# Linear attention and a two-layer network in one kernel: where block 0's first part ends

## The chip, the cores and the metric

One core of a Trainium2 chip runs the kernel. The metric is the device time of one execution in microseconds (us), median of the runs; lower is better. Engines are named as the profile names them: PE is TensorE (its matmuls; PEld its weight loads), DVE is VectorE, ACT is ScalarE, POOL is GpSimd, SP issues the DMAs.

## The reference

The kernel computes attention with exponential feature maps and feeds its output to a two-layer network. For 8 batches of 8 heads, 576 tokens and a head width of 64:

```python
def phi(x):
    proj = np.einsum('bhsd,df->bhsf', x, w_phi)
    proj = proj - np.max(np.abs(proj), axis=-1, keepdims=True)
    return np.concatenate([np.exp(proj), np.exp(-proj)], axis=-1)
q_p, k_p = (phi(q), phi(k))
kv = np.einsum('bhsf,bhsd->bhfd', k_p, v)
z = np.sum(k_p, axis=2)
num = np.einsum('bhsf,bhfd->bhsd', q_p, kv)
den = np.einsum('bhsf,bhf->bhs', q_p, z)[..., None] + 1e-06
x = (num / den).transpose(0, 2, 1, 3).reshape(B * S, H * D)
h = x @ w_in
g = np.maximum(0.01 * h, h)
return g @ w_out
```

The network has 4608 tokens, a width of 512 and 2048 hidden features. w_in and w_out arrive as 64-bit floats.

## The kernel before, in words

**Attention** goes by head pairs, i = 4 x batch + pair, 32 in all. A pair has a k phase (k_phase: projections, exponentials, the matrix kv) and a q phase (token_q_phase for pairs 4 to 7, q_phase from 8 on: projections, exponentials, numerator and denominator, division). The result is written to `ring`, which holds two batches. The last step of a pair's q phase is POOL's multiplication `ring<-ring,mb`. Pairs 0 to 3 (batch 0) have functions of their own that run first. From pair 4 on the generator `attention()` gives the k phase of pair i and the q phase of pair i - 1 in turns, and `advance(goal)` draws from it.

**The network** works on 18 blocks of 256 tokens. `split(i)` copies a block out of `ring` in two parts, xh on ACT and the rest xl on POOL; both tiles exist once, so a block's split waits until layer 1 of the block before it has been read. A step (i, ft) is block i with one of 16 weight groups of 128 hidden features: `layer1` has 12 matmuls of 256 columns (L601, L602, L604; w0h and w0l are the two parts of w_in), then ACT and DVE make gh and gl (L607, L69, L609), and `layer2` has 6 matmuls of 512 columns into two accumulators (L623 to L625, w1h and w1l for w_out). Layer 2 is written three steps behind layer 1 (LAG). Tokens 0 to 575 are batch 0, so blocks 0 and 1 need batch 0 alone, block 2 needs pairs 4 to 7 and block 4 (tokens 1024 to 1279) pairs 8 to 11.

**The weights** are prepared on the chip by `load_weights`: 32 pieces of 512 KB, w_in and w_out in turns by group, are loaded, turned from 64-bit to 32-bit numbers and split in two parts by DVE, ACT and copies (L160 to L169). The last step of a piece is `w0l<-ql,w0h` or `w1l<-ql,w1h` on DVE (L74).

**Order.** Block 0 is cut in two. Its first CUT steps come first, then the 16 steps of block 1, then the rest of block 0, then blocks 2 to 17. After the first part `layer2` copies the two half sums from the accumulators to a tile (held, tag ks, L629 to L633), and after the last part they are added (L636). The lines that set this:

```python
steps = [(i, ft) for i in range(2, NBLK) for ft in range(NFT)]
steps = [(0, ft) for ft in range(CUT)] + [(1, ft) for ft in range(NFT)] + [(0, ft) for ft in range(CUT, NFT)] + steps
split(0)
for n, (i, ft) in enumerate(steps):
    layer1(i, ft)
    advance(min(room(n // NFT + 1), NP * (1 + (n + 1) / NFT * T / S) + 2))
    if n + 1 < len(steps) and steps[n + 1][0] != i:
        advance(math.ceil((steps[n + 1][0] + 1) * T / S) * NP)
        split(steps[n + 1][0])
    if n >= LAG:
        layer2(*steps[n - LAG])
```

The order on each engine is not that of the code. A scheduler orders the instructions when the program is built, by priorities: batch 0 first (PF, PU), then the rest of attention (PA), then the weights (PW), then the network (0). Each engine then runs its list strictly in that order, so an instruction that waits holds up all behind it.

Of the kernel before, what the change touches and what calls it, by code (L numbers as in the profile page):

```python
# [27 lines left out]
NTOK = B * S  # L28
NBLK = NTOK // T
LAG = 3  # L30
CUT = 8
NN = 8
NK = 8
NF = 12
# [12 lines left out]
def attention_moe_kernel(ctx: ExitStack, tc: tile.TileContext, q, k, v, vt, w_phi, w_in, w_out, out):  # L47
# [538 lines left out]
    def split(i):  # L586
        for d in range(NP):
            t0 = 0
            while t0 < T:
                c = (i * T + t0) % (2 * S)  # L590
                n = min(T - t0, S - c % S)
                x = ring[:, c // S, d, c % S : c % S + n]
                t1 = t0 + n
                copy_("xh", xh[:, d, t0:t1], x)
                tt_("xl", xl[:, d, t0:t1], x, xh[:, d, t0:t1].bitcast(F32), ALU.subtract)
                t0 = t1
# [17 lines left out]
    def layer2(i, ft, half=range(TT)):  # L614
        first, last = (ft in (0, CUT), ft in (CUT - 1, NFT - 1)) if i == 0 else (ft == 0, ft == NFT - 1)
        if first and half[0] == 0:
            for t in range(TT):
                accs[i, t] = pt("acc")
        gh, gl = gs[i, ft]
        for t in half:  # L620
            ts = slice(t * P, t * P + P)
            a = accs[i, t]
            nc.tensor.matmul(a, lhsT=gh[:, ts], rhs=weight(1, "h", ft), start=first, stop=False)  # L623
            nc.tensor.matmul(a, lhsT=gh[:, ts], rhs=weight(1, "l", ft), start=False, stop=False)  # L624
            nc.tensor.matmul(a, lhsT=gl[:, ts], rhs=weight(1, "h", ft), start=False, stop=last)  # L625
        if not last:
            return
        for t in half:
            if ft == CUT - 1:  # L629
                if t == 0:  # L630
                    held[0] = st([P, TT, DM], F32, "ks")
                copy_("o", held[0][:, t], accs[i, t])
                continue  # L633
            o = st([P, DM], F32, "ek" if i == NBLK - 1 and t else "o")
            if i == 0:
                nc.vector.tensor_tensor(o, accs[i, t], held[0][:, t], op=ALU.add)  # L636
            else:
                copy_("o", o, accs[i, t])
            r = i * T + t * P
            nc.sync.dma_start(out[r : r + P, :], o)  # L640
# [29 lines left out]
# [3 lines that stand above are left out]
# [47 lines left out]
```

## Time and profile before

| | before |
|---|---|
| median of 3 runs | 1194.11 us (1193.7 to 1196.47) |
| profiled execution | 1196.45 us, its span 1194.7 us |
| PE busy | 1164.5 us, 97% |
| DVE busy | 755.9 us, 63% |
| ACT busy | 833.5 us, 70% |
| POOL busy | 417.5 us, 35% |
| mean granted PE clock | 0.994 |

The times are those of one profiled execution unless said otherwise. A row of a timeline gives start, length, engine, line, operation and tiles (output<-inputs), and in brackets how long the engine had been idle and what ended that. A row of the stage windows gives the busy time of each engine in a stretch, with the number of instructions, the granted clock of PE (1.00 is full), the share of the DMA engines and GB/s. Line 69, 71 or 74 is that of a helper that records copies and two-input operations, so there the tile says what is meant.

### The profile page before, as it was taken

The page shows a single profiled execution, that of the slowest core. Times are in us where ns is not written, and L with a number is a line of the kernel's source. Part 1 is how long each engine was busy: PE and PEld are TensorE (multiplying, and loading weights), DVE is VectorE, ACT ScalarE, POOL GpSimd, SP SyncE. Part 2 cuts the span into 40 slices and gives each one's busy share as a digit, 9 for nine tenths or more (in the row PEclk, how much of TensorE's full clock was granted, in tenths as well). Part 3 has the DMA queues.
Part 4 walks back from the last instruction along what each step waited for, and adds up shares of the span by engine and source line. Part 5 has one row for each costly group of instructions (what it writes and reads, how often), then busy time and mean ns, then how long its engine had stood idle before and what let it go on. Part 6 is the DMA issues. An engine that isn't in the chain of part 4 may idle for free.

```text
span 1194.7 us, 21190 instructions
## 1 busy us (share of the span) xinstructions
PE 1164.5 (97%) x7576; PEld 1045.5 (88%) x7576; DVE 755.9 (63%) x1510; ACT 833.5 (70%) x2108; POOL 417.5 (35%) x422
## 2 busy tenths in 40 slices
PE   8899999999998999999999999999999999999998
PEld 5687888899897989889899999998999999988987
DVE  4899883566767777677787777726777776111111
ACT  4898884667777787878788888837787877432232
POOL 0111011345454444545455454604454544110000
PEclk9899999999998999999999999999999999999999
DMA  7334532111201111110111111101011100000000
GB/s 208 90 101 142 152 114 59 40 42 31 60 22 50 32 50 31 41 30 22 50 31 50 32 49 32 49 12 37 23 50 32 49 1 19 1 18 19 1 19 18
DMA packets 62778, 57.01 MB, mean 48 GB/s; under 512 B 45136, under 2 KB 46288, under 8 KB 62672
## 3 DMA queue, kind: packets, MB, share of 16 engines
q1 hardware_dynamic: 62672, 55.65, 16.4%
q8 instruction: 60, 0.98, 0.4%
q14 instruction: 46, 0.38, 0.1%
HBM read 46.20 MB, written 9.44 MB: 47 GB/s over the span
## 4 chain that ended last, share of the span: by engine, by line
PE 82%; DVE 8%; ACT 5%; issue 2%; DMA 1%; POOL 1%; SPq 0%; DVEq 0%; ACTq 0%; POOLq 0%
PE h L601 10%; PE h L604 10%; PE h L602 10%; PE acc L623 10%; PE acc L625 10%; PE acc L624 10%; PE c L211 7%; PE a L302 2%; PE a L420 2%; PE a L418 2%; PE a L417 2%; PE a L231 2%; PE a L333 1%; PE a L377 1%; PE a L378 1%
## 5 line engine op out<-in xcount | busy, mean ns | idle before, releaser
L601 PE MATMUL h<-xh,w0h 128*128 128x256 f32 x1152 | 296.3, 287 | 5.9 <-DVE gl L609 4.9
L602 PE MATMUL h<-xh,w0l 128*128 128x256 f32 x1152 | 290.9, 282 | 0.0
L609 DVE TENSOR_TENSOR gl<-h,gh 128x256 fp32r<-128x256 f32 x288 | 118.7, 416 | 245.9 <-ACT gh L69 220.6
L623 PE MATMUL acc<-w1h,gh 128*128 128x512 f32 x576 | 229.6, 399 | 6.4 <-ACT gh L69 6.3
L601 PEld LDWEIGHTS h<-xh,w0h 128*128 128x128 f32 x1152 | 218.0, 189 | 17.0 <-DVE gl L609 8.0
L624 PE MATMUL acc<-w1l,gh 128*128 128x512 f32 x576 | 227.7, 395 | 0.0
L602 PEld LDWEIGHTS h<-xh,w0l 128*128 128x128 f32 x1152 | 217.9, 189 | 7.0 <-issue 0.4
L607 ACT ACTIVATE h<-h 128x256 f32<-128x256 f32 x288 | 105.3, 368 | 155.0 <-PE h L604 152.0
L625 PE MATMUL acc<-w1h,gl 128*128 128x512 f32 x576 | 204.4, 396 | 0.0
L604 PE MATMUL h<-xl,w0h 128*128 128x256 f32 x1152 | 200.3, 283 | 0.0
L74 POOL TENSOR_TENSOR ql<-eq,qh 128x576 fp32r<-128x576 f32 x96 | 146.5, 1539 | 73.6 <-ACT qh L69 51.0
L604 PEld LDWEIGHTS h<-xl,w0h 128*128 128x128 f32 x1152 | 164.5, 189 | 1.1 <-issue 0.4
L74 POOL TENSOR_TENSOR kpl<-ek,kph 128x512 fp32r<-128x512 f32 x72 | 96.6, 1342 | 146.9 <-PE c L211 67.2
L623 PEld LDWEIGHTS acc<-w1h,gh 128*128 128x128 f32 x576 | 108.4, 188 | 27.7 <-ACT gh L69 8.9
L624 PEld LDWEIGHTS acc<-w1l,gh 128*128 128x128 f32 x576 | 108.4, 188 | 18.0
L69 ACT CAST gh<-h 128x256 fp32r<-128x256 f32 x288 | 105.1, 371 | 25.6 <-PE acc L624 20.0
L74 POOL TENSOR_TENSOR xl<-ring,xh 128x256 fp32r<-128x256 f32 (+3 forms) x100 | 62.6, 655 | 162.1 <-PE h L604 131.6
L74 POOL TENSOR_TENSOR ring<-ring,mb 128x576 f32<-128x576 f32 (+2 forms) x45 | 49.8, 1108 | 192.9 <-DVE mb L559 39.2
L625 PEld LDWEIGHTS acc<-w1h,gl 128*128 128x128 f32 x576 | 99.3, 189 | 8.1
L249 ACT ACTIVATE ek<-pmk 128x256 f32<-128x256 f32 (+1 forms) x128 | 53.3, 417 | 33.5 <-POOL kpl L74 17.3
L199 DVE TENSOR_TENSOR ks<-rk,ks 64x576 fp32r<-64x576 f32 x40 | 44.5, 1112 | 30.5 <-ACT ks L69 29.9
L211 PE MATMUL c<-kph,vh 128*66 128x256 f32 x240 | 62.1, 281 | 0.7 <-ACT kph L69 0.7
(214 smaller groups left out, 2257.8 us busy)
## 6 DMA issues: line engine op xcount, KB each, us to landing
out_dram<-o SPq DMA_DIRECT2D x35, 256.0 KB, 2.1
rk<-in_k_dram SPq DMA_DIRECT2D x29, 288.0 KB, 2.8
ring<-in_w_in_dram SPq DMA_DIRECT2D x16, 512.0 KB, 3.6
qh<-in_w_out_dram SPq DMA_DIRECT2D x16, 512.0 KB, 3.7
rq<-in_q_dram SPq DMA_DIRECT2D x28, 288.0 KB, 3.0
rv<-in_v_dram SPq DMA_DIRECT2D x29, 256.0 KB, 3.5
rv<-in_vt_dram SPq DMA_DIRECT2D x58, 32.0 KB, 3.0
fr<-in_k_dram SPq DMA_DIRECT2D x2, 288.0 KB, 3.4
```

Source lines behind the costliest of these rows:

```text
L69: nc.scalar.copy(o, i)
L74: (nc.vector if pick(key) == "v" else nc.gpsimd).tensor_tensor(o, a, b, op=op)
L211: nc.tensor.matmul(kvp[0 : lt.shape[1], 256 * j : 256 * j + 256], lhsT=lt, rhs=rt, start=first and j == 0, stop=last, skip_group_check=True)
L249: nc.scalar.activation(ek[r, :, 0:F], pmk[r, 2 * s : 2 * s + 2], AF.Exp)
L601: nc.tensor.matmul(ph, lhsT=weight(0, "h", ft)[:, d * P : d * P + P], rhs=xh[:, d], start=d == 0, stop=False)
L602: nc.tensor.matmul(ph, lhsT=weight(0, "l", ft)[:, d * P : d * P + P], rhs=xh[:, d], start=False, stop=False)
L604: nc.tensor.matmul(ph, lhsT=weight(0, "h", ft)[:, d * P : d * P + P], rhs=xl[:, d], start=False, stop=d == NP - 1)
L607: nc.scalar.activation(ph, ph, AF.Prelu, alpha=0.01)
L609: nc.vector.tensor_tensor(gl, ph, gh.bitcast(F32), op=ALU.subtract)
L623: nc.tensor.matmul(a, lhsT=gh[:, ts], rhs=weight(1, "h", ft), start=first, stop=False)
L624: nc.tensor.matmul(a, lhsT=gh[:, ts], rhs=weight(1, "l", ft), start=False, stop=False)
L625: nc.tensor.matmul(a, lhsT=gl[:, ts], rhs=weight(1, "h", ft), start=False, stop=last)
```

## The change

Block 0's first part has twelve weight groups instead of eight:

```diff
-CUT = 8
+CUT = 12
```

The steps are the same 288. Before they went (0,0) to (0,7), (1,0) to (1,15), (0,8) to (0,15), (2,0) and on. Now they go (0,0) to (0,11), (1,0) to (1,15), (0,12) to (0,15), (2,0) and on. The half sums are put aside after group 11 instead of 7. The scheduler makes a new order of it on every engine; PE's is the same up to the end of (0,7) and again from head pair 25 on.

On PE, behind (0,7), stood the first step of block 1 (w0h_616 is the tile of w_in's groups 0 to 3, w1h_721 that of w_out's groups 4 to 7), layer 2 of an earlier step, and soon the next step:

```order
L604 MATMUL h<-xl,w0h_616 128x256 x4
L623 MATMUL acc<-w1h_721,gh 128x512
L624 MATMUL acc<-w1l_722,gh 128x512
L623 MATMUL acc<-w1h_721,gh 128x512
L624 MATMUL acc<-w1l_722,gh 128x512
L211 MATMUL c<-kpl,rv 66x256 x2
L601 MATMUL h<-xh,w0h_616 128x256
```

Now the step there is (0,8) (w0h_800, w1h_813: groups 8 to 11), and this stands between it and (0,9):

```order
L211 MATMUL c<-kpl,rv 66x256 x2
L320 MATMUL a<-ident,tq 128x128 x4
L302 MATMUL a<-bd,rk 128x256
L211 MATMUL c<-ek,rv 66x256 x2
L623 MATMUL acc<-w1h_813,gh 128x512 x2
L333 MATMUL a<-qs,kvh 128x256 x4
L302 MATMUL a<-bd,rq 64x256
L624 MATMUL acc<-w1l_814,gh 128x512
L625 MATMUL acc<-w1h_813,gl 128x512
L624 MATMUL acc<-w1l_814,gh 128x512
L625 MATMUL acc<-w1h_813,gl 128x512
L601 MATMUL h<-xh,w0h_800 128x256
```

Before, two steps of block 1 were two attention matmuls apart; now two steps of block 0 are ten attention matmuls and four transposes apart, and both layers use weight groups that are just being prepared.

On POOL, where block 4 is split (xl in pieces of 128x128, eight in all) and pair 11 ends with `ring<-ring,mb`, the list was:

```order
L74 TENSOR_TENSOR xl<-ring,xh 128x128 x4
L74 TENSOR_TENSOR kpl<-ek,kph 128x512
L74 TENSOR_TENSOR xl<-ring,xh 128x128 x3
L74 TENSOR_TENSOR ql<-eq,qh 128x576 x2
L74 TENSOR_TENSOR pmk<-pmk,m_3647 64x256
L74 TENSOR_TENSOR ring<-ring,mb 128x576
L74 TENSOR_TENSOR xl<-ring,xh 128x128
```

Now it is:

```order
L74 TENSOR_TENSOR pmk<-pmk,m_3647 64x256
L74 TENSOR_TENSOR ring<-ring,mb 128x576
L74 TENSOR_TENSOR vl<-rv,vh 128x512
L74 TENSOR_TENSOR vl<-rv,vh 64x128
L181 MEMSET rv 128x10x2
L74 TENSOR_TENSOR xl<-ring,xh 128x128 x4
L74 TENSOR_TENSOR kpl<-ek,kph 128x512
L74 TENSOR_TENSOR xl<-ring,xh 128x128 x4
```

Seven of the eight pieces stood ahead of the end of pair 11, and one behind it; now all eight stand behind it, with the next pair's work between.

## Prediction

> **What bounds the kernel now.** I read the page first, for the engine that is busy throughout:
>
> ```profile
> PE 1164.5 (97%) x7576; PEld 1045.5 (88%) x7576; DVE 755.9 (63%) x1510; ACT 833.5 (70%) x2108; POOL 417.5 (35%) x422
> PEclk9899999999998999999999999999999999999999
> ```
>
> TensorE (PE) is busy for 97% of the span. The change adds and removes no arithmetic, so the time can move only where PE stops, or where its clock is granted less than in full. After the start, such a stop stands in the thirteenth digit of the clock. The stage windows (PE, PEld, DVE, ACT and POOL busy, granted clock, DMA share) show that place and the stage that the change rearranges:
>
> ```profile
> 90.00:120.00 30.00, 28.96 (x164) 23.66 (x163) 27.87 (x54) 25.39 (x60) 5.91 (x7) 1.00 0.50 143
> 120.00:150.00 30.00, 29.91 (x174) 24.62 (x173) 27.04 (x59) 24.48 (x58) 1.18 (x3) 1.00 0.53 153
> 150.00:180.00 30.00, 30.00 (x181) 25.02 (x180) 25.96 (x55) 24.46 (x64) 5.28 (x8) 1.00 0.37 104
> 180.00:210.00 30.00, 30.00 (x175) 25.14 (x174) 9.48 (x24) 14.54 (x40) 3.62 (x7) 1.00 0.22 60
> 210.00:240.00 30.00, 30.00 (x189) 26.38 (x188) 15.76 (x32) 18.62 (x52) 9.13 (x14) 1.00 0.16 43
> 330.00:360.00 30.00, 30.00 (x201) 27.22 (x199) 20.32 (x41) 23.98 (x64) 16.19 (x19) 1.00 0.09 22
> 360.00:390.00 30.00, 25.00 (x151) 22.43 (x149) 20.52 (x43) 22.13 (x57) 13.93 (x14) 0.89 0.17 50
> 390.00:420.00 30.00, 30.00 (x209) 27.77 (x208) 22.43 (x46) 22.58 (x58) 12.33 (x11) 1.00 0.12 31
> ```
>
> Two stages count. From 90 to 180 us VectorE (DVE) is busy 26 to 28 of 30 us with the preparation of the weights, while PE stays nearly full. From 360 to 390 us PE is busy only 25.00 of 30 us, at a mean clock of 0.89, and runs 151 matmuls where its neighbours run 201 and 209. The chain of waits there (start, length, engine, tile, line), and PE's own rows (idle time in brackets), name the cause:
>
> ```profile
> 367.18 1.42 POOL ring L74
> 368.63 0.31 ACT xh L69
> 368.98 0.38 PE h L601
> ```
>
> ```profile
> 362.45 0.43 PE L420 MATMUL a<-ql,kvh 128*128 128x288 f32 x2
> ...
> 365.80 0.40 PE L377 MATMUL a<-qs,wq 128*128 128x288 f32 x1 [1.13 <-DVE tq L379]
> ...
> 367.98 0.40 PE L377 MATMUL a<-qs,wq 128*128 128x288 f32 x1 [1.64 <-DVE pmk L236]
> ...
> 375.29 0.50 PE L623 MATMUL acc<-w1h,gh 128*128 128x512 f32 x1 [1.91 <-ACT gh L69]
> ```
>
> Block 4 is the first block that needs the last head pair of batch 2 (pair 11). Its final attention matmul (L420) starts at 362.45, its normalised output is written by GpSimd (POOL) at 367.18, and only then can the last piece of xh be copied and layer 1 go on at 368.98: 6.5 us. Meanwhile PE has only a few attention matmuls left, and idles in the three pieces of the rows, and the lower clock falls into the same window.
>
> **The gain: the stop at block 4.** The row of 360 to 390 us prices it: 5.0 us idle, and (1 - 0.89) x 30 = 3.3 us of lost clock, together 8.3 us. As a check, 54 matmuls fewer than the neighbours' mean of 205 per 30 us are 7.9 us. In the new order pair 11 stands earlier against the blocks. Its last L420 is PE row 1266, and the first L601 of block 4 is row 1349 (before: 1334 and 1301, so that block 4 had begun with pair 11 unfinished). Between the two new rows stand 45 layer-1 and 25 layer-2 matmuls, 24 attention matmuls of the fast form and four small transposes. The prices are in the chain of waits from 100 to 115 us, where PE is the chain, and in PE's rows:
>
> ```profile
> 103.48 0.23 PE acc L624
> 105.00 0.47 PE h L604 x4
> 105.93 1.73 PE a L333 x8
> 107.66 1.73 PE a L302 x8
> ```
>
> ```profile
> 100.70 0.60 PE L320 MATMUL a<-ident,tq 128*128 128x128 f32 x4
> 101.14 0.41 PE L281 MATMUL c<-ident,ek 66*128 66x66 f32 x4
> ...
> 110.76 0.47 PE L601 MATMUL h<-xh,w0h 128*128 128x256 f32 x1
> 111.07 0.28 PE L602 MATMUL h<-xh,w0l 128*128 128x256 f32 x1
> ```
>
> Layer 1 costs 0.12 us a matmul, layer 2 0.23, a plain fp32 attention matmul 0.43 (two records of 0.216; the order counts one), a 128x128 transpose 0.11 (100.70 to 101.14, by four). So 69 x 0.12 + 25 x 0.23 + 0.2 = 14.2 us of PE work lie between pair 11 and block 4, against the 6.5 us that the chain took: 7.7 us to spare, and the stop goes whole. What is late next is nothing that waits on attention: later batches too stand earlier in the new order, and from pair 25 on both orders are the same, so what PE lost or won by then stays to the end.
>
> **The cost: waiting for weights.** Steps (0,8) to (0,11) now come directly behind (0,7), while their weights are still being made. These DVE rows give the times, and the pitch of what moves:
>
> ```profile
> 112.03 0.64 DVE L74 TENSOR_TENSOR w0l<-ql,w0h 128x512 fp32r<-128x512 f32 x1
> ...
> 118.44 0.69 DVE L71 COPY ks<-acc 128x512 f32<-128x512 f32 x1
> ...
> 133.90 0.68 DVE L239 TENSOR_REDUCE m<-a 128x4 f32<-128x512 f32 x1
> ...
> 138.85 0.39 DVE L609 TENSOR_TENSOR gl<-h,gh 128x256 fp32r<-128x256 f32 x1
> 139.16 0.78 DVE L74 TENSOR_TENSOR w0l<-ql,w0h 128x512 fp32r<-128x512 f32 x1
> ```
>
> The first and last row are the w0l of groups 8 and 11, done at 112.7 and 139.9 us. In the new DVE order up to group 11 there are three gl fewer (0.31 each, from its row to the next), the copy of block 0's half sum has moved behind (0.69), and one attention reduction more has come in (0.68): 0.93 + 0.69 - 0.68 makes group 11 ready 0.9 us earlier, at 139.0. The (1,0) of before began at 110.76; in its place stands (0,8), with one layer 2 of six matmuls more ahead of it (1.4 us), so at 112.1, just when its weights are there. From the first matmul of (0,8) to that of (0,11) the new PE order holds 36 layer-1 (4.3 us), 18 layer-2 (4.1), 28 plain fp32 matmuls of 256 columns (12.0) and four of 64 (0.9), ten transposes (1.1) and four small ones (0.2): 22.6 us. Six times an MoE matmul follows attention, and the first then takes 0.31 us instead of 0.12 (110.76 to 111.07): 1.1 us. PE has 23.7 us to do in 139.0 - 112.1 = 26.9 us: it idles for 3.2 us. The nearest row of such a wait is 0.6 us:
>
> ```profile
> PE h L601 <- ACT w0h L69: 0.6, 1, 0.6
> PE h L601 <- DVE gl L609: 4.9, 4, 1.8
> ```
>
> The bounds are 0.6 below (this row, if DVE gets through faster) and 8.4 us above, the three MoE steps (12 x 0.12 + 6 x 0.23 = 2.8 us each) that PE did in this stretch and no longer can, if attention fills none of it. I take 2.5 us, between the row and the count. A fourth change of block was not added: there are still three splits in the first 33 steps. The last two now lie four steps apart instead of eight, each refilling xh and xl, single buffers; before, the two splits fell between 177 and 226 us, where the rows above show PE busy 30.00 of 30 us, since layer 2 lags by three steps and covers the refill with attention. I cost this at nothing; without that cover the nearest row is the stop at block 4. On SP's queue the loads keep their order but for neighbours: nothing.
>
> Does the wait lower the clock? In the rows above the clock of 0.89 came with idle pieces of at most 1.91 us. The Trainium skill, "TensorE: Matmul & The Clock Gate", section "Why this matters for your kernels", says that only idle gaps of over about 3 us drop the clock. This trace disagrees: 1.13 and 1.64 us were enough. By the rule the 2.5 us in pieces would never cost clock; by the trace half of the clock loss seen at 360 us (3.3 us) could come with them, 1.7 us, which I put in the range.
>
> **The sum.** -8.3 + 2.5 = -5.8 us. The profiled execution took 1196.45 us (span 1194.70 and 1.75 around it) and would take 1190.65. The median of the runs is 1194.11, 2.3 us lower, so I take the difference from that: 1188.3 us.
>
> **The rivals.** *The forecast*, 0.55: the stop goes, a short wait for weights comes.
>
> *Attention gets no faster*, 0.25. The new order lets attention run ahead from 112 us on; on the chip it may be held by DVE, which is busy for nine tenths of the time there. Then PE idles for the 8.4 us above, pair 11 ends when it did, and block 4 comes 8.4 us later to it: the stop of 8.3 us is used up by the idle time ahead of it. Net 0, 1194. For it speaks DVE's 27.0 of 30 us; against it, that the order of attention's DVE work moved ahead of the weights' by only one reduction.
>
> *Slower: waits and clock together*, 0.14. As the last, with each of the three weight periods also bringing such a clock loss of 1.7 us: 8.4 + 3 x 1.7 - 8.3 = +5.2, 1199.3. It decides from 11.9 us of waits and clock on (8.3 and 3.6, which is 0.3% of the time and about what a measurement can tell from no change). Against it speaks that the same alternation of weight waits and attention ran from 80 to 105 us with no pause above 0.6 us.
> The Trainium skill, "Perfetto Trace Analysis", section "Optimization Strategy", advises interleaving stages with different limits, and this change takes interleaving away from the DVE-bound stage. That rule is this rival; the trace's full PE at 120 to 180 us agrees with it so far.
>
> *More goes than the stop*, 0.06. Attention ahead of the blocks also spares PE the waits of L601 on gl (4.9 us in four pieces, row above), and weights cost 0.6: -8.3 - 4.9 + 0.6 = -12.6, 1181.5.
>
> **How the numbers follow.** The likeliest case gives 1188.3; its own bounds are -8.3 + 0.6 and -8.3 + 2.5 + 1.7 with 1 us of leftovers at block 4, so 1186.4 to 1191. The range goes on to most of the other cases, from 1182 to 1197. Faster by over 0.3% (below 1190.5): 0.55 and 0.06 less what the forecast's upper edge gives away, and some of the second: 0.60. Within 0.3%: 0.26. Slower (above 1197.7): 0.14.
>
> **What would show it.** Right: PE busy near 30 of 30 us and clock 1.00 in all windows from 340 to 400 us; in POOL's rows all of block 4's xl after pair 11's ring; new PE rows waiting on w0h, w0l, w1h or w1l between 112 and 142 us, 2 to 3 us in sum. Wrong: a wait of PE on attention's DVE or on xh elsewhere with a digit of the clock below 9; over 8 us of waits ahead of 142 us; or idle time at the two splits four steps apart.

## The result

The changed kernel takes 1201.72 us (median of 4 runs, 1200.76 to 1202.88), the kernel before 1193.9 in the same comparison: a ratio of 1.0061, 95% interval 1.0044 to 1.0079. It is slower, and 4.7 us above the top of the range. The profiled execution took 1202.88 us, its span 1201.1. The page of the profile after, PE's line and the granted clock:

```profile
PE 1167.0 (97%) x7576; PEld 1043.3 (87%) x7576; DVE 769.1 (64%) x1510; ACT 832.0 (69%) x2108; POOL 417.8 (35%) x422
PEclk9899999999999999999999999999999999999999
```

The low digit at block 4 is gone. The stage windows after, in the columns of the prediction, agree:

```profile
120.00:150.00 30.00, 27.57 (x157) 21.80 (x155) 28.94 (x61) 26.84 (x68) 6.29 (x8) 1.00 0.50 142
...
330.00:360.00 30.00, 30.00 (x211) 27.82 (x210) 20.27 (x42) 22.13 (x56) 12.76 (x12) 1.00 0.08 20
360.00:390.00 30.00, 29.25 (x200) 26.48 (x199) 21.86 (x42) 25.89 (x70) 14.79 (x17) 1.00 0.18 50
```

From 360 to 390 us PE runs 200 matmuls instead of 151, with 0.75 us idle instead of 5.0 and no clock lost. The price stands at 120 to 150 us: 2.43 us idle, where it was 0.09. So far the trace is close to the forecast, and the kernel should be some 5 us ahead. It nearly is: the first layer-1 matmul of block 6 starts at 494.5 us, before at 498.6. Block 11 starts at 816.1, before at 809.5. The whole loss, 10.7 us, therefore lies between, in a stretch that the prediction costs at nothing. The window from 540 to 810 us (blocks 7 to 10) in the trace of before, and then in that of after:

```profile
540.00:810.00 270.00, 268.13 (x1839) 246.91 (x1838) 186.62 (x360) 210.31 (x536) 127.48 (x116) 1.00 0.13 36
```

```profile
540.00:810.00 270.00, 261.05 (x1757) 237.03 (x1756) 185.35 (x347) 199.10 (x505) 120.23 (x107) 0.99 0.13 35
```

PE idles for 8.95 us instead of 1.87, and runs 82 matmuls fewer. PE's waits in that window after (total, times, longest):

```profile
PE c L211 <- ACT kph L69: 4.4, 3, 3.4
PE a L417 <- ACT qh L69: 2.2, 4, 0.8
PE c L211 <- POOL kpl L74: 1.0, 1, 1.0
PE h L601 <- DVE gl L609: 0.9, 1, 0.9
```

In the trace of before, the same view lists one wait of PE from 540 to 820 us:

```profile
PE h L601 <- DVE gl L609: 1.8, 1, 1.8
```

The first two waits after are for copies on ACT, which before had none there (kph is the first part of the exponentials of the keys and kpl the rest; qh is the same for the queries). The timeline of all engines shows the longest, a few us behind the begin of block 7 at 560.7 (L607 is the network's Prelu, L405 and L406 are the exps of the queries, L249 one of the keys; L398 subtracts the maximum, L400 transposes):

```profile
563.28 2.83 DVE L398 TENSOR_TENSOR tq<-tq,m 128x576 f32<-128x576 f32 x2
...
563.68 1.81 POOL L74 TENSOR_TENSOR kpl<-ek,kph 128x512 fp32r<-128x512 f32 x1
...
565.52 0.42 ACT L249 ACTIVATE ek<-pmk 128x256 f32<-128x256 f32 x1 [0.42 <-POOL kpl L74]
...
566.03 0.76 DVE L400 STREAM_TRANSPOSE mb<-tq 128x576 f32<-128x576 f32 x1
566.83 0.44 ACT L405 ACTIVATE eq<-mb 128x288 f32<-128x288 f32 x1 [0.58 <-DVE mb L400]
567.17 0.43 ACT L406 ACTIVATE eq<-mb 128x288 f32<-128x288 f32 x1
...
568.17 0.63 ACT L607 ACTIVATE h<-h 128x256 f32<-128x256 f32 x2
...
568.74 0.60 ACT L69 CAST kph<-ek 128x512 fp32r<-128x512 f32 x1
...
569.39 0.33 PE L211 MATMUL c<-kph,vh 128*66 128x256 f32 x1 [3.40 <-ACT kph L69]
```

It is read upwards. PE waits for kph. On ACT, kph stands behind both Prelus of the new block, these behind four exps, and the first of these waited for DVE's transpose, which stood behind L398. The Prelus' sums were finished by 565.2 us. Both layer-1 buffers (tag h) thus stay full, layer 2 of the old block is used up, and the next matmul in PE's list is the one that needs kph.

### The profile page after: what moved, and what is told of

It reads as the page before. It is cut to its first block, busy times and chain, and to the rows that moved or that the text cites. A ratio compares the mean times of both kernels' runs of the same rounds, so it can differ in the third digit from the quotient of the medians.

```text
span 1201.1 us, 21195 instructions
## 1 busy us (share of the span) xinstructions
PE 1167.0 (97%) x7576; PEld 1043.3 (87%) x7576; DVE 769.1 (64%) x1510; ACT 832.0 (69%) x2108; POOL 417.8 (35%) x422
## 4 chain that ended last, share of the span: by engine, by line
PE 72%; DVE 7%; ACT 6%; issue 3%; POOL 0%; DVEq 0%; ACTq 0%; POOLq 0%
PE h L601 9%; PE acc L623 9%; PE h L602 9%; PE h L604 9%; PE acc L624 9%; PE acc L625 9%; PE c L211 5%; PE a L417 2%; PE a L418 2%; PE a L420 2%; PE a L231 2%; PE a L302 1%; PE a L333 1%; PE a L377 1%; PE a L378 1%
## 5 line engine op out<-in xcount | busy, mean ns | idle before, releaser
L607 ACT ACTIVATE h<-h 128x256 f32<-128x256 f32 x288 | 105.0, 368 | 158.3 <-PE h L604 156.2
L625 PE MATMUL acc<-w1h,gl 128*128 128x512 f32 x576 | 201.9, 396 | 0.0
L74 POOL TENSOR_TENSOR ql<-eq,qh 128x576 fp32r<-128x576 f32 x96 | 143.4, 1507 | 97.3 <-ACT qh L69 70.1
L69 ACT CAST gh<-h 128x256 fp32r<-128x256 f32 x288 | 104.8, 371 | 28.4 <-PE acc L624 24.2
L74 POOL TENSOR_TENSOR xl<-ring,xh 128x256 fp32r<-128x256 f32 (+3 forms) x100 | 66.7, 697 | 157.4 <-PE h L604 138.3
L249 ACT ACTIVATE ek<-pmk 128x256 f32<-128x256 f32 (+1 forms) x128 | 53.3, 416 | 38.4 <-POOL kpl L74 18.7
L74 POOL TENSOR_TENSOR vl<-rv,vh 128x512 fp32r<-128x512 f32 (+1 forms) x48 | 46.9, 976 | 55.2 <-ACT vh L69 36.8
```

Source lines behind the costliest of these rows:

```text
L69: nc.scalar.copy(o, i)
L74: (nc.vector if pick(key) == "v" else nc.gpsimd).tensor_tensor(o, a, b, op=op)
L249: nc.scalar.activation(ek[r, :, 0:F], pmk[r, 2 * s : 2 * s + 2], AF.Exp)
L607: nc.scalar.activation(ph, ph, AF.Prelu, alpha=0.01)
```

## The experiments

**How losses are counted.** The loss of a block is the elapsed time from the first layer-1 matmul two steps ahead of its begin to that 14 steps behind, less PE's work between them by its order (matmuls times the pitches in the prediction, with a digit more); clock counts as loss. "Weights" is the same from step 8 to step 37, and "all" from the start to the last step. The *place* of a block is the PE work, by the order, between the first q projection (L377) of the pair begun last and the block's first layer-1 matmul. Two pairs are worked on per block, so a place repeats from block to block.

| kernel | weights | 4 | 5 | 6 | 7 | 8 | 9 | 10 | all | median us |
|---|---|---|---|---|---|---|---|---|---|---|
| before | 5.4 | 10.5 | 2.2 | 3.1 | 3.1 | 0.7 | 0.7 | 0.7 | 58.6 | 1193.9 |
| after | 8.8 | 2.0 | 2.2 | 3.6 | 6.7 | 2.2 | 4.6 | 3.1 | 65.0 | 1201.72 |
| e1_hold70 | 8.8 | 2.1 | 2.6 | 1.5 | 0.7 | 0.8 | 0.7 | 0.7 | 49.2 | 1186.29 |
| e2_cut9 | 6.5 | 12.0 | 1.8 | 1.5 | 0.7 | 0.8 | 0.7 | 0.7 | 55.8 | 1193.01 |
| e3_cut13 | 10.1 | 2.4 | 5.0 | 1.2 | 4.5 | 3.1 | 2.0 | 2.7 | 60.0 | 1198.33 |
| e4_cut14 | 14.8 | 3.3 | 3.0 | 2.6 | 4.0 | 3.3 | 4.8 | 2.3 | 67.7 | 1206.45 |
| e5_hold72 | 8.3 | 2.0 | 0.8 | 9.1 | 1.8 | 3.0 | 1.7 | 0.7 | 58.4 | 1196.26 |
| e6_cut11_hold70 | 9.5 | 4.5 | 4.6 | 5.4 | 2.0 | 4.6 | 2.8 | 1.2 | 69.2 | 1205.32 |
| e7_cut11_hold71 | 8.2 | 3.3 | 1.5 | 7.6 | 0.7 | 0.8 | 0.7 | 0.7 | 58.5 | 1196.14 |
| e8_short_vl | 9.3 | 2.0 | 2.2 | 3.5 | 6.4 | 2.2 | 2.6 | 2.8 | 60.2 | 1198.48 |
| e9_o_dve | 8.6 | 2.4 | 2.9 | 1.6 | 0.8 | 0.8 | 0.8 | 0.7 | 54.4 | 1192.24 |
| e10_xl_half_dve | 11.0 | 2.9 | 0.9 | 3.5 | 2.9 | 2.9 | 2.9 | 2.8 | 61.6 | 1199.4 |
| e11_xh_dve | 7.8 | 6.2 | 6.1 | 9.4 | 1.2 | 2.3 | 4.8 | 2.5 | 80.8 | 1216.0 |
| e12_short_sub | 8.1 | 2.0 | 2.2 | 2.1 | 5.1 | 4.2 | 4.1 | 1.7 | 58.5 | 1199.2 |
| e13_good_then_bad | 8.5 | 2.0 | 2.6 | 1.5 | 2.0 | 0.9 | 5.7 | 2.6 | 64.7 | 1203.71 |
| e14_good_then_mixed | 8.8 | 2.0 | 2.6 | 1.5 | 2.0 | 8.3 | 1.5 | 1.8 | 67.2 | 1203.65 |
| e15_prelu_first | 8.4 | 2.0 | 2.1 | 3.5 | 5.6 | 5.6 | 1.8 | 2.9 | 62.3 | 1199.95 |
| e16_gh_first | 8.2 | 2.0 | 2.1 | 3.5 | 3.1 | 2.1 | 0.7 | 0.7 | 54.7 | 1191.79 |

A value of 0.7 or 0.8 is the floor of this count and no loss: e1_hold70 has it at blocks 7 to 10, where PE does not idle. Each row is one execution, while the runs of one kernel differ by 0.7 to 4.8 us, so a difference of 1 or 2 us in one row alone says little. "All" takes in clock lost ahead of 60 us, which came in some executions (0.89 from 30 to 60 us in the trace of before) and not in others (1.00 in that of e12_short_sub).

After less before: weights +3.4, block 4 -8.5, blocks 5 to 10 +11.9, the rest -0.4, together +6.4, which is the difference of the spans (the medians differ by 7.8). The 10.7 us above are less than the 11.9 because the new order also holds 1.0 us less of PE's work between the starts of blocks 6 and 11. The places explain where to look: blocks 5 to 10 lie at 2.8, 5.4, 5.2, 7.5, 6.4 and 7.1 us before, at 13.1, 12.3, 11.3, 13.1, 12.3 and 10.8 us after.

**First round: is it the place?** The first kernel keeps twelve groups and holds attention back once, by queueing on PE the attention matmuls of one round (pair 14's k phase, pair 13's q phase) behind the layer 1 of step 70, (4,6). The changed offset leaves the order as it was.

```diff
+HOLD = (14, 70)
...
-            state["n"] = max(state["n"], next(stream, B * NP))
+            if HOLD and HOLD[0] - 1 <= state["n"] < HOLD[0] and HOLD[1] in marks:
+                with tc.issue_after(marks[HOLD[1]]):
+                    state["n"] = max(state["n"], next(stream, B * NP))
+            else:
+                state["n"] = max(state["n"], next(stream, B * NP))
...
-        advance(min(room(n // NFT + 1), NP * (1 + (n + 1) / NFT * T / S) + 2))
+        marks[n] = gs_last[0]
+        advance(min(room(n // NFT + 1), NP * (1 + (n + 1) / NFT * T / S) + 1))
```

> Twelve groups, and from head pair 14 on attention's matmuls are held behind layer 1 of step 70, (4,6), once: that sets the start of every later q phase about 7 us of PE work ahead of the next block's first step (as in the kernel before) instead of 11 to 13. Theory A (the 12.4 us lost at blocks 7 to 10 come from the place in attention's cycle at which a block begins): the losses at blocks 7 to 10 fall to those of the kernel before, the early gain of 5 to 6 us stays, and the time is 1188 to 1191 us, ratio to before 0.994 to 0.998. Rival B (the later losses belong to twelve groups as such, by chance of the new lists, wherever attention stands): they stay, 1199 to 1204 us.

Measured: 1186.29 us (1185.3 to 1187.0), ratio to before 0.9933 (0.9917 to 0.995). It beats both kernels, and is 1.7 us faster than the range of theory A. Its places from block 5 on are 6.4 to 7.2 us; the weights and block 4 lose what they lose in the changed kernel. The window of blocks 7 to 10:

```profile
540.00:810.00 270.00, 270.00 (x1859) 249.38 (x1858) 188.56 (x366) 210.48 (x532) 128.01 (x117) 1.00 0.13 36
```

PE does not idle at all there. The other three change the number of groups alone:

```diff
-CUT = 12
+CUT = 9
```

> Nine groups ahead of block 1. In its order the q phases start 6.4 to 7.3 us of PE work ahead of blocks 5 to 10. Theory A: no loss at blocks 7 to 10 beyond that of before (a few tenths each); weights cost under 1 us; the stop at block 4 may be there or not: 1186 to 1195 us. Rival B: any reshuffle of the lists loses several us at blocks 7 to 10: 1199 or more.

> Thirteen groups. The q phases start 10.8 to 13 us of PE work ahead of blocks 6 to 10, as with twelve. Theory A: the same kind of losses at blocks 7 to 10 as with twelve, 8 to 14 us over before there, and about one step more of waiting for weights: 1200 to 1207 us. Rival B: no statement on where; anything from 1190 to 1207.

> Fourteen groups. The q phases start 26 to 28 us of PE work ahead of blocks 5 to 10, that is, near the end of a pair's cycle of about 31. Theory A has no earlier measure for this place: it expects the cost at blocks 5 to 10 to be about equal from block to block, since the place is; two steps more of waiting for weights than twelve (3 to 6 us). 1190 to 1208 us. Rival B: costs that differ at random from block to block.

Measured against the same runs of before (1193.67 us): nine groups 1193.01 us, ratio 0.9996 (0.9986 to 1.0005); thirteen 1198.33, 1.0041 (1.0028 to 1.0054); fourteen 1206.45, 1.0105 (1.009 to 1.012). Nine groups lie at 6.4 to 7.3 us, and lose 6.2 us at blocks 5 to 10 (e1_hold70 7.0), but still have the stop at block 4 (12.0 us). Thirteen and fourteen lie at 10.8 to 15.9 and at 25 to 28 us and lose 18.5 and 20.0 us there, and each further group costs more waiting for weights (10.1, 14.8 us). Nine and fourteen groups took a time within their ranges. Thirteen took 1.7 us less than its range: blocks 7 to 10 lose 7.1 us more than before, where 8 to 14 were expected.

**Second round: the place with the number of groups fixed.** The hold two steps later; eleven groups with the hold behind step 70, and with it behind step 71; and the changed kernel without part of a POOL operation. The two with eleven groups differ by one number:

```diff
-HOLD = (14, 70)
+HOLD = (14, 71)
```

> Twelve groups and the hold of e1_hold70, but behind step 72 instead of 70. By the order the place (PE work between the first q projection of the last pair begun and the block's first layer-1 matmul) becomes 29.4, 26.1, 2.8, 2.8, 5.4 and 7.5 us at blocks 5 to 10, where e1_hold70 had 7.2, 6.4, 7.1, 6.6, 7.1 and 6.6. Theory A (the place of the attention's cycle at which a block begins sets what the block's start loses): what other kernels lost at the nearest places (3.2 at 26 to 28, 2.2 at 2.8, 3.1 at 5.4, 0.7 at 7.5) sums to 14.6 us against e1_hold70's 7.0, so 1193.9 us, 1190 to 1197. Rival C (the hold itself gains, because attention runs later and out of the way, whatever the place): no slower than e1_hold70, 1184 to 1187 us.

> Eleven groups and the hold behind step 70; the pair with e7_cut11_hold71, which differs by one number. Places 11.3, 11.3, 12.4, 10.8, 13.1 and 12.7 us at blocks 5 to 10. Theory A: about 3.3 us lost at each of the six (the mean of the changed kernel and of e3_cut13 at 10.8 to 13.1), 19.6 in all, about 1198.5 us (1194 to 1202), 12 us behind e7_cut11_hold71. Rival C (a hold gains as such) and rival D (the number of groups sets the time, by the waits for weights): within 2 us of e7_cut11_hold71.

> Eleven groups and the hold behind step 71. Places 0.3, 3.7, 7.1, 6.6, 7.1 and 6.6 us at blocks 5 to 10. Theory A: 2.2, 2.5 and four times 0.7, 7.5 us in all, so about 1186.5 us (1184 to 1190), 12 us ahead of e6_cut11_hold70. Rivals C and D: within 2 us of e6_cut11_hold70.

Measured: e5_hold72 1196.26 us, ratio 1.0014 (1.0005 to 1.0024); e6_cut11_hold70 1205.32, 1.009 (1.0075 to 1.0105); e7_cut11_hold71 1196.14, 1.0013 (1.0004 to 1.0022). What a hold brings depends on its step: two steps later it is worth 10.0 us less than in e1_hold70, and one step is worth 9.2 us with the same groups (forecast 12; rivals C and D within 2). The sums were off: e5_hold72 lies in its range, but e6_cut11_hold70 3.3 us and e7_cut11_hold71 6.1 us above theirs. At blocks 7 to 10 the places do as forecast (0.7 to 0.8 each in e7_cut11_hold71, 1.2 to 4.6 in e6_cut11_hold70). But block 6, the first or second behind the hold, lost 9.1 us in e5_hold72 and 7.6 in e7_cut11_hold71, where 3.2 and 2.5 were expected. The place alone does not price a block.

```diff
-            for r, c in ((slice(0, P), slice(0, 8)), (slice(64, P), slice(8, 10))):
+            for r, c in ((slice(0, P), slice(0, 8)), (slice(64, P), slice(8, 10)))[18 <= i < 26:]:
```

> The changed kernel, with the first of the two POOL subtractions that make vl (128 partitions by 512) left out for pairs 18 to 25, which are begun in blocks 7 to 10; the tile then holds the values of pair 17. PE's, ACT's and SP's orders stay and the places too (11.3 to 13.1 us). Theory A1 (POOL's row of vl, four xl and kpl at a block's start holds back the exps and so ACT's list): about 2 us of that row is gone at each of the four block starts, the 16.6 us lost at blocks 7 to 10 fall by half or more, 1190 to 1196 us. Theory A2 (ACT's list waits for DVE's maximum chain, with POOL beside it only): the loss stays, 1199 to 1203 us.

Measured: 1198.48 us (1197.75 to 1200.13), ratio 1.0038 (1.0024 to 1.0052). Blocks 7 to 10 lose 14.0 us instead of 16.6, and block 7 keeps its stop, here in PE's waits from 540 to 820 us:

```profile
PE c L211 <- ACT kph L69: 3.9, 2, 3.1
```

The time lies between the ranges of the two theories. The part of vl that was left out is not what gates block 7; kpl, which POOL runs beside L398, was still there, so POOL as a whole is not ruled out.

**Third round: other edits that move the place, and DVE.** The table of engines, with copies of layer 2's sums on DVE (first), every second xl on DVE (second) and xh on DVE (third):

```diff
-ENG = {..., "o": "av", ..., "l": "v"}
+ENG = {..., "o": "v", ..., "l": "v"}
+ENG = {..., "o": "av", ..., "l": "v", "xl": "pv"}
+ENG = {..., "o": "av", ..., "l": "v", "xh": "v"}
```

> The changed kernel (twelve groups, no hold) with all copies of layer 2's sums on DVE instead of ACT and DVE in turn. This moves the places too: 6.7, 6.4, 6.6, 6.6, 6.6 and 6.6 us at blocks 5 to 10, by another edit than the hold. Theory A (the place sets what a block's start loses): as e1_hold70, about 7 us lost at blocks 5 to 10 instead of 22.4, 1186.5 us (1184 to 1190). Rival C (the hold gains as such, the place is not it): without a hold this stays near the changed kernel, 1198 to 1203 us.

> The changed kernel with every second subtraction of a block's xl on DVE instead of POOL. Places 7.5, 7.1, 7.1, 7.1, 7.1 and 7.1 us at blocks 5 to 10, and 6.0 at block 4. Theory A: 1.5 at blocks 5 and 6 and 0.7 at the next four, 5.8 us in all, and 1 to 2 more than the changed kernel at block 4: about 1187 us (1184 to 1191). Rival C: near the changed kernel, 1198 to 1203 us.

> The changed kernel with the four xh copies of a block's start on DVE instead of ACT. Places 9.6, 10.6, 13.4, 12.8, 12.4 and 13.0 us at blocks 5 to 10, so the blocks begin where those of the changed kernel do. Theory A: 3 us lost at each, about 1199 us (1195 to 1204). Rival E (what counts is ACT's load at a block's start, and any edit that takes work off ACT or POOL there gains as much as e9_o_dve and e10_xl_half_dve): 1184 to 1191 us.

Measured: 1192.24 us, ratio 0.999 (0.9981 to 1.0); 1199.4, 1.0056 (1.0041 to 1.0071); 1216.0, 1.0192 (1.0176 to 1.0207). All three are above the ranges of theory A, by 2.2, 8.4 and 12.0 us. The first loses 0.7 to 0.8 us at each of blocks 7 to 10 without any hold, as forecast, and rival C (1198 to 1203) fails; the rest of the forecast gain went 2.4 us ahead of block 4 and 2.8 us behind block 11. The second lies at 7.1 us, where 0.7 was expected, and loses 2.8 to 2.9 us at each; its time is in the range of rival C. PE's waits from 540 to 820 us name a new link, the copy of layer 2's sums on ACT:

```profile
PE c L211 <- ACT o L69: 4.3, 4, 1.1
```

The third lies at 12.4 to 13.4 us there and loses 10.8 us, near the 12 expected; with more on DVE it loses still more at blocks 5 and 6 (15.5 us). So moving work between engines moves the loss, and a good place need not stay good when work moves.

```diff
-            nc.vector.tensor_tensor(tj, tj, m[:, j].unsqueeze(2).broadcast_to([P, 18, 32]), op=ALU.subtract)
+            w = 2 if 17 <= i < 25 else 18; nc.vector.tensor_tensor(tj[:, 0:w], tj[:, 0:w], m[:, j, 0:w].unsqueeze(2).broadcast_to([P, w, 32]), op=ALU.subtract)
```

> The changed kernel with DVE's subtraction of the maximum cut from 18 to 2 of its 18 pieces of 32 columns, for the queries of pairs 17 to 24 (the other pieces keep their values), which lie in blocks 7 to 10. Places stay bad: 10.8, 12.3, 13.6 and 13.6 us at blocks 7 to 10. Theory A2 (PE stops since ACT's list stands at the exps behind DVE's subtraction and transpose, with the new block's Prelu behind them): about 2 us less of DVE work ahead of mb, and the stop of 3.4 us with its half clock goes: the 16.6 us lost at blocks 7 to 10 fall to 8 or less, 1191 to 1196 us. If DVE does not gate it (POOL, or PE's own order does): 1199 to 1203 us.

Measured: 1199.2 us, ratio 1.0047 (1.0032 to 1.0062). The long wait for kph went (its longest is now 0.7 us), but blocks 7 to 10 still lose 15.1 us. The scheduler had reordered the lists for the shorter instruction, and PE's waits from 540 to 820 us turned into others:

```profile
PE h L601 <- DVE gl L609: 2.1, 3, 0.9
PE c L211 <- POOL kpl L74: 0.7, 1, 0.7
PE c L211 <- ACT kph L69: 0.7, 1, 0.7
```

The expected 8 us or less did not come, and the time is in the range for the case that DVE does not gate the stop, though the stop went. As the lists changed too, this run settles neither.

**Fourth round: a good kernel made bad again.** e1_hold70 with a second hold, of the next pairs, behind step 116 and behind step 118:

```diff
-HOLD = (14, 70)
+HOLDS = ((14, 70), (18, 116))
...
-        advance(min(room(n // NFT + 1), NP * (1 + (n + 1) / NFT * T / S) + 1))
+        advance(min(room(n // NFT + 1), NP * (1 + (n + 1) / NFT * T / S) + (1 if n < 90 else -1)))
```

> e1_hold70 with a second hold, of the attention of the next two pairs behind step 116. The orders are those of e1_hold70 up to the end of block 6; from there attention pauses for five steps and then runs at places 12.4, 12.0 and 12.5 us at blocks 8, 9 and 10 (7.1, 6.6, 7.1, 6.6 at blocks 7 to 10 in e1_hold70). Theory A (the place sets the loss, as long as each engine has its own work): 2 to 5 us lost at each of blocks 8 to 10 as in the changed kernel at 12.3 to 13.1 (mean 3.3), 10 in sum instead of 2.2, and something at the pause itself: about 1195 us (1192 to 1200). Rival F (the loss came from what stood before block 7, and stays away once that is mended): 0.7 at each, 1185 to 1189 us and only the pause's cost on top.

> The same second hold behind step 118: places 6.1, 10.3 and 7.2 us at blocks 8, 9 and 10. Theory A: 0.7 to 1.5 at block 8, about 3 at block 9, 0.7 to 1.5 at block 10, 5 in sum, so 4 to 6 us ahead of e13_good_then_bad: about 1190 us (1187 to 1195). Rival F: as e13_good_then_bad within 2 us.

Measured: 1203.71 us, ratio 1.0086 (1.0069 to 1.0103), and 1203.65, 1.0084 (1.0065 to 1.0103). Up to block 6 both lose what e1_hold70 loses. Then the loss comes back, so it is not a matter of what stood earlier. In the first it is 9.2 us at blocks 8 to 10 (10 expected), but unevenly: block 8, at the bad place of 12.4 us, loses only 0.9, where 2 to 5 were expected. The delayed attention also costs 8.6 us more than in e1_hold70 behind block 11, which had not been counted, and the time is 3.7 us above theory A's range. In the second the forecast failed: block 8, at the good place of 6.1 us right behind the pause, loses 8.3 us instead of 1, as this stage window shows:

```profile
600.00:630.00 30.00, 26.32 (x154) 23.13 (x153) 20.10 (x36) 21.75 (x56) 17.12 (x15) 0.89 0.17 49
```

Block 11 then loses some 6 us more than in e1_hold70, and the time is 8.7 us above the range. The two kernels agree within 2 us, as rival F said, but both are some 15 us above its times.

**Fifth round: the order on ACT alone.** In e1_hold70's ACT rows around block 7 (begin 558.0 us; its line numbers are higher by one from L69 on, by three at the network: L610 is the Prelu, L406 the exp) the Prelus stand ahead of the exps:

```profile
560.77 0.62 ACT L70 CAST kph<-ek 128x512 fp32r<-128x512 f32 x1
561.30 0.37 ACT L610 ACTIVATE h<-h 128x256 f32<-128x256 f32 x1
...
564.06 0.63 ACT L70 CAST kph<-ek 128x512 fp32r<-128x512 f32 x1
...
565.28 0.37 ACT L610 ACTIVATE h<-h 128x256 f32<-128x256 f32 x1
565.62 0.45 ACT L406 ACTIVATE eq<-mb 128x288 f32<-128x288 f32 x1
```

In the changed kernel the exps stand first. The last two kernels are the changed kernel with that turned round, at the same place of block 7 (11.3 us): the exps queued behind the second Prelu, and behind its gh copy.

```diff
+BEHIND = {18: 7, 20: 8, 22: 9, 24: 10}
...
         nc.scalar.activation(ph, ph, AF.Prelu, alpha=0.01)
+        prelu[i, ft] = nc.cur_bb.bb.instructions[-1]
         copy_("gh", gh, ph)
...
+                if j == 0 and i in BEHIND:
+                    with tc.issue_after(prelu[BEHIND[i], 1]):
+                        nc.scalar.activation(eq[:, 0], mb[:, u], AF.Exp)
+                        nc.scalar.activation(eq[:, 1], mb[:, u], AF.Exp, scale=-1.0)
```

In e16_gh_first the line that sets prelu[i, ft] stands behind the copy gh. Both also lower the offset in advance from 2 to -1 from step 90 on, which by itself leaves the order as it was.

> The changed kernel with the first four exps of the queries of pairs 18, 20, 22 and 24 queued on ACT behind the Prelu of the second step of blocks 7, 8, 9 and 10. Up to there every order is the changed kernel's. The two Prelus now stand ahead of the exps, but the copy kph that PE waits for, and the copies gh that free the layer-1 buffers, still stand behind them. Places 11.3, 12.0, 12.5 and 7.3 us at blocks 7 to 10. Theory G (PE stops because kph and gh stand behind exps that wait for DVE): block 7 still loses 6 us or more, and the whole takes 1196 to 1202 us. Theory H (the Prelus alone are what is late): block 7 loses 2 to 3 us, 1191 to 1195 us.

> The same, with the exps queued behind the copy gh of the second step. On ACT stand now two Prelus, kph, two pmk copies and two gh, then the four exps; on PE layer 2 of the new block follows the kph matmuls. Places 11.3, 11.3, 6.6 and 7.3 us at blocks 7 to 10. Theory G: the stop of 3.4 us shrinks to 1.5 (kph then waits for ek's exps alone) and its stretch of half clock goes, so block 7 loses about 2.5 us instead of 6.7 at the same place, blocks 9 and 10 about 0.7 by their places, and the whole takes 1190 to 1195 us. If PE's stop has another cause: block 7 loses 6 us as before, 1194 to 1199 us.

Measured: e15_prelu_first 1199.95 us (1199.85 to 1200.58), ratio 1.0056 (1.004 to 1.0073); e16_gh_first 1191.79 (1189.57 to 1192.38), ratio 0.998 (0.9971 to 0.9989). In e15_prelu_first kph still stands behind the exps (L613 is the Prelu, L408 and L409 are the exps):

```profile
564.24 0.63 ACT L613 ACTIVATE h<-h 128x256 f32<-128x256 f32 x2
564.92 0.44 ACT L408 ACTIVATE eq<-mb 128x288 f32<-128x288 f32 x1
...
566.27 0.60 ACT L70 CAST kph<-ek 128x512 fp32r<-128x512 f32 x1
```

Its PE row of the stop:

```profile
566.92 0.34 PE L212 MATMUL c<-kph,vh 128*66 128x256 f32 x1 [2.84 <-ACT kph L70]
```

In e16_gh_first kph and gh stand ahead of them:

```profile
565.38 0.63 ACT L613 ACTIVATE h<-h 128x256 f32<-128x256 f32 x2
565.94 0.61 ACT L70 CAST kph<-ek 128x512 fp32r<-128x512 f32 x1
...
566.97 0.66 ACT L70 CAST gh<-h 128x256 fp32r<-128x256 f32 x2
567.50 0.48 ACT L408 ACTIVATE eq<-mb 128x288 f32<-128x288 f32 x1
```

And PE's row:

```profile
566.59 0.33 PE L212 MATMUL c<-kph,vh 128*66 128x256 f32 x1 [1.38 <-ACT kph L70]
```

The stop went from 3.40 to 2.84 and 1.38 us (1.5 forecast), and block 7's loss from 6.7 to 5.6 and 3.1 us (6 or more, and 2.5, forecast); both times lie in theory G's ranges. Some of that loss is clock: 0.94 from 570 to 600 us in the changed kernel, 0.96 from 540 to 570 us in e15_prelu_first, 1.00 in both windows of e16_gh_first. By the traces, the lists of PE, DVE and POOL are those of the changed kernel until behind the stop, and ACT's up to the exps. At one place, with the same work on every engine, the order on ACT decides the stop of block 7. The gain of the whole kernel over the changed one also has another source: behind block 8 the places became 6.6 and 7.3 us, where blocks 9 and 10 lose 0.7 us each.

## Why the prediction was wrong

**The gain at block 4** was right in mechanism and size: -8.3 forecast, -8.5 by the count. In POOL's list pair 11's last step now ends before the split:

```profile
355.56 1.43 POOL L74 TENSOR_TENSOR ring<-ring,mb 128x576 f32<-128x576 f32 x1 [4.83 <-DVE mb L429]
...
363.66 1.89 POOL L74 TENSOR_TENSOR xl<-ring,xh 128x128 fp32r<-128x128 f32 x4 [3.80 <-PE h L604]
```

**The wait for weights** was put at 2.5 us; the count gives +3.4, and PE's rows from 112 to 145 us show 2.4 us of it in four pieces:

```profile
124.17 0.73 PE L623 MATMUL acc<-w1h,gh 128*128 128x512 f32 x2 [1.19 <-ACT gh L69]
131.16 1.05 PE L211 MATMUL c<-ek,rv 128*66 128x256 f32 x4 [0.82 <-issue]
140.09 1.08 PE L211 MATMUL c<-kpl,rv 128*66 128x256 f32 x4 [0.17 <-ACT kpl L250]
144.32 0.38 PE L604 MATMUL h<-xl,w0h 128*128 128x256 f32 x1 [0.24 <-POOL xl L74]
```

The size was near, the mechanism was not: none is put down to a weight tile (for the piece of 0.82 us the profile names no releaser). The largest waits for the network's own gh, which had to queue on ACT behind two instructions of the weights' conversion:

```profile
122.38 0.38 ACT L607 ACTIVATE h<-h 128x256 f32<-128x256 f32 x1
122.68 0.61 ACT L69 CAST w1h<-ql 128x512 fp32r<-128x512 f32 x1
123.18 0.67 ACT L165 ACTIVATE kvl<-ring 128x512 int32<-128x512 uint32 x1
123.76 0.36 ACT L69 CAST gh<-h 128x256 fp32r<-128x256 f32 x1
```

No clock went with these pieces in this execution (1.00 at 120 to 150 us), so the 1.7 us held in reserve were not needed; that is luck, as the last section shows.

**The step that failed** is the one that cost the stretch behind block 4 at nothing: "What is late next is nothing that waits on attention: later batches too stand earlier in the new order, and from pair 25 on both orders are the same, so what PE lost or won by then stays to the end." What PE lost by pair 25 was never counted. Attention that runs earlier against the blocks also meets each block's begin at another point of its cycle, and at block 7 ACT's list then holds exps that wait for DVE ahead of copies that PE needs. Blocks 5 to 10 lose 11.9 us more, 11.4 of them at blocks 7 to 10 and 3.6 at block 7 alone. None of the listed signs of being wrong showed it: the weights' waits stayed under 8 us, PE did not idle at the two splits, and the clock's digits on the page stayed at 9. Had these blocks lost what they did before, the forecast would have stood: -8.5 + 3.4 - 0.4 = -5.5 us, against -5.8; e1_hold70, in which they lose 3.5 us less than before, takes 1186.29.

**The rivals.** Attention did get faster. "Slower: waits and clock together" had the sign and nearly the time (1199.3), but not the cause: the weights cost 3.4 us, not 8.4 plus clock. The interleaving advice of the Trainium skill ("Perfetto Trace Analysis", section "Optimization Strategy"), which stood beside that rival, is borne out for the weights with 3.4 us and does not bear on the 11.9.

**What stays open.** In the counts above, 22 of the 29 block begins at places of 6.1 to 7.5 us in blocks 7 to 10 lose 0.7 or 0.8 us, and those at other places 0.9 to 6.7. The seven that do not fit lie in e10_xl_half_dve (four, with another division of the work), in e14_good_then_mixed (two, behind the pause) and in e15_prelu_first (block 10). Blocks 5 and 6 lose 0.9 to 3.5 us even at such places. So the place goes with the loss, but does not price it by itself. That the order on ACT is the cause was shown for block 7 alone. For blocks 8 to 10 it stays open: PE's waits there in the changed kernel are of 0.3 to 1.0 us, on kph, qh, kpl and gl, and at block 8 of e16_gh_first the same reordering, at a place of 11.3 us, left 2.1 us where the changed kernel has 2.2.

## What to carry to other kernels

When a change lets a periodic stage run earlier, the point at which it meets the other stage's boundaries shifts everywhere behind, not only where the stop was: compare the new order at several later boundaries on the engine whose copies release PE, not on PE alone. At such a boundary look for instructions in an in-order list that wait for another engine ahead of those that free PE's buffers, and queue them behind all of these: queued behind the Prelus alone they left a stop of 2.84 us here, behind the copies one of 1.38. A hold of one round made a loss of 0.6% a gain of 0.7%. And give each stretch behind the repaired stop a price of its own, with a bound, before calling the gain kept.

## What the runs showed of the hardware

L398, a DVE operation on two tiles, can take more than twice as long when POOL works beside it. All of its 48 instances after, and the two in the stop (shortest, median and longest in ns):

```profile
L398 DVE TENSOR_TENSOR tq<-tq,m x48: 745/759/1849, 241.7 to 1016.2; 128x576 f32<-128x576 f32 x48
```

```profile
L398 DVE TENSOR_TENSOR tq<-tq,m x2: 1056/1451/1846, 563.3 to 564.3; 128x576 f32<-128x576 f32 x2
```

In the trace of before, 44 of the 48 take 744 to 764 ns; the four others take 1203 to 1878, each while POOL runs kpl. In the stop POOL's kpl takes 1.81 us from 563.68 to 565.49, against 1.29 at 569.47, and the second L398 ends 0.6 us behind it (563.28 + 2.83 = 566.11). That looks like each waiting for the other to end. The Trainium skill ("SBUF — State Buffer", section "SBUF: two separate sides") says that a DVE operation with two SBUF inputs and a GpSimd operation that reads SBUF lock a shared pair of ports for a whole instruction; these rows agree. The 1.3 us that the two L398 took longer (2.83 against twice 0.75) stand in the chain that stopped PE. What the stop would be without kpl beside them was not tried.

The clock does not go by the length of a stop alone. In the changed kernel PE's stop of 1.19 us at 124.17 left the window of 120 to 150 us at 1.00. In e8_short_vl, whose orders are the same up to 520 us, the same stop of 1.19 us at 121.71 went with 0.94:

```profile
120.00:150.00 30.00, 28.38 (x151) 22.38 (x150) 28.31 (x60) 26.57 (x67) 6.81 (x9) 0.94 0.49 140
```

A stop of 2.84 us in e15_prelu_first went with 0.96, while the 1.38 us of e16_gh_first left 1.00:

```profile
540.00:570.00 30.00, 26.58 (x166) 22.93 (x165) 23.99 (x46) 22.60 (x59) 15.37 (x15) 0.96 0.17 49
```

```profile
540.00:570.00 30.00, 28.01 (x187) 24.63 (x187) 24.27 (x46) 23.51 (x61) 15.24 (x15) 1.00 0.17 49
```

The 1.8 us wait of before from 540 to 820 us left it at 1.00 too (its row of 540 to 810 us). So a stop of over 1 us can cost clock or not, and what decides was not found out. The Trainium skill's rule in the prediction ("TensorE: Matmul & The Clock Gate", section "Why this matters for your kernels", no idle gaps of over about 3 us) is thus no safe bound here: 1.19 us were enough once.
